# A gated mix of two attentions, forward and backward: who asks for the sweep's chunks in the backward weave, and what is loaded before it

## The chip, the core and the metric

The kernel runs on one core of one Trainium2 chip. The core has TensorE (PE, with PEld for its weight loads), VectorE (DVE), ScalarE (ACT), GpSimd (POOL) and SyncE (SP); SP issues most of the transfers here, GpSimd the rest. The metric is the device time of one execution in microseconds; the time of a kernel is the median of its runs.

## The reference

Two attention layers read the same input x (2048 tokens of 576), and a gate mixes them:

```python
g = sigmoid((x * gate_w).sum(-1, keepdims=True))
a = A(x)     # 32 query heads of 18, one shared key and value head, softmax over all 2048 keys, output projection
b = B(x)     # recurrent: segments of 32 tokens with 8 memory tokens ahead of them, 32 heads of 128
out = g * a + (1 - g) * b
```

In B each segment attends over its own 32 tokens (causal) and the 8 memory tokens; the first 8 rows of its output are the memory of the next of the 64 segments. The kernel returns the output and the gradients, for a given gradient of the output, of x, of the weights of A and B, of the first memory and of the gate: a forward pass and a full backward pass.

## The kernel before, in words

The program is one long sequence of stages: preparation and projections; a forward weave of B's recurrence with A's first pass; the token stage `b_bulk` (from about 2010 to 2604 us), which does attention and its gradients for B's own tokens; the backward weave (2604 to 4272 us); then `b_post`, the weight gradients `b_dw` and `a_final`. The order of the instructions on each engine is the order in which the program writes them (`manual_schedule`).

The backward weave is what the change is about. `weave` (L302 to 318) interleaves two generators. `a_pass2`, the sweep, goes over A's second pass in 1024 units (4 blocks of 512 keys, 256 units each). A unit is two score matmuls (`b_S`), an exponential on ScalarE (`b_E`), two gradient matmuls (`b_dP`), two products on VectorE (`b_dS`) and the accumulation into `b_acc`. Four units share one chunk of queries and output gradients, `b_QS`, 128 x 1024 values of bf16 (256 KB), loaded from `qs_dram`; there are 256 chunks in three buffers, `QS[c % 3]`. `load(c)` is written in the step n = 4c - 6 (L2107), and the chunk is first read by `mm_S(4c)`, which is written in step 4c - 1, five steps later. The first two chunks are loaded in the token stage by `sweep_first` (L2048), called at step `t == NG - 8`.

`b_chain_bwd`, the chain, goes backwards through B's 64 segments, with 16 yields in each, so 16 units and 4 chunks of the sweep run per segment. A segment needs the upstream rows `r_dOm` (from `dm` and the weights `WoT`), the spread probabilities `r_PqB` (from `r_pT` by `pad_in`, `pad_T` and `blocks`), loads of its own (`load_a`, `load_b`, `load_c`, on SP), and 24 weight pieces `WT` and the `WoT` pieces that stay in SBUF. It also computes, four blocks per segment, the key and value gradients of the token stage (`kv_load`, `kv_blk`, `kv_mm`, `kv_out`), whose results GpSimd stores (`dvx_dram`, `dkx_dram`, L1157). GpSimd also stores `pq_dram` (L1101), `dOm_dram` (L1198), `dTm_dram` (L1273), `dmT_dram` (L1174) and `dxr_dram` (L1318), and prepares blocks (`r_kb`, `r_dSB`, `r_dSqB`, `r_PqB`, `r_prod`, `r_hx`, `r_dspad`) that TensorE and VectorE read.

The weave begins with 12 lead steps of the sweep alone. At the lead steps named in `prime`, here 2 and 5, one piece of the chain is run too: step 2 runs the chain up to its first yield (buffers zeroed, `load_a` and `load_b` of the last segment), step 5 up to the second (`load_c`, with `r_dx` and `r_q`). What follows the second yield, `pad_in`, `r_PqB`, and in the last segment the zeroing of `r_dOm` and `x_rows`, comes after the lead. Each step also draws one item of `early`, here `bwd_weights` (L678): weight pieces 12 to 23, then the four `WoT` pieces and their tail, on SP. The pieces 0 to 11 are loaded in the token stage into the ring buffers that its own loads no longer need (`load`, L705).

Of the kernel before, what the change touches and what calls it, by code (L numbers as in the profile page):

```python
# [12 lines left out]
BF16 = mybir.dt.bfloat16  # L13
# [3 lines left out]
P = 128  # L17
# [5 lines left out]
E = 128  # L23
# [23 lines left out]
class Kern:  # L47
# [628 lines left out]
        self.WoT = (pool.tile([P, 4, J], BF16, name="WoT"), pool.tile([P, 4, 512], BF16, name="WoTt"))  # L676

    def bwd_weights(self, pool):  # L678
        for j in range(12, 24):
            self.load_WT(j, pool)  # L680
            yield
        for kt in range(4):
            self.nc.sync.dma_start(self.WoT[0][:, kt, :], self.st_WoT[kt])
            yield
        self.nc.sync.dma_start(self.WoT[1][:], self.st_WoTt[:])
        yield
# [6 lines left out]
    def b_bulk(self, wp, vp, kp, sp, psum):  # L693
        nc = self.nc
# [5 lines left out]
        NG = NTT * 8  # L700
        NC = NTT * 2

        self.WT = {}

        def load(c, names):  # L705
            if c >= NC:
                for w in names:
                    if w in deep and len(self.WT) < 12:
                        self.load_WT(len(self.WT), w=w)
                return  # L710
            tt, h0 = c // 2, 16 * (c % 2)
            d = C.setdefault(c, {})
            for w in names:
                if w == "mT":
                    if c % 2 == 0:
                        mT[tt] = {}
                        for x in ("k", "v"):
                            mT[tt][x] = kp.tile([P, 4, HB, 8], BF16, name=f"x_{x}mT", bufs=2)
                            nc.sync.dma_start(mT[tt][x][:], self.mTd[x][4 * tt:4 * tt + 4].rearrange("s p h t -> p s h t"))
                elif w in ("kB", "vB"):  # L720
                    for i in range(4):
                        nc.sync.dma_start(
                            mB[w[0]][c % 2][32 * i:32 * i + 32, :, i, :],
                            self.mtok[w[0]][tt * 32:(tt + 1) * 32, h0 * P:h0 * P + 2048]
                            .rearrange("r (g i e) -> r g i e", i=4, e=E)[:, :, i, :])
                else:
                    if w in deep:
                        d[w] = self.ring(w)[:, 0:2048].rearrange("p (h e) -> p h e", e=P)
                    else:
                        d[w] = vp.tile([P, 16, P], BF16, name=f"x_{w}", bufs=3)[:]  # L730
                    nc.sync.dma_start(d[w].rearrange("p h e -> p (h e)"),
                                      self.xtok[w][tt * P:(tt + 1) * P, h0 * P:h0 * P + 2048])

        deep = self.RING
# [229 lines left out]
        for t in range(NG + 6):  # L964
            if t == NG - 8:
                self.sweep_first()
            sc["D"] = psum.tile([P, 512], F32, name="x_D", bufs=1)
            sc["Sb"] = psum.tile([P, 512], F32, name="x_S", bufs=1)
            for n, st in order:
                if n is None:  # L970
                    st(t)
                    continue
                if 0 <= t - n < NG:
                    st(t - n)
                if st in after and t - n >= 0 and (t - n) % 4 == 3:
                    c = (t - n) // 4
                    for w, wait in after[st]:
                        later.setdefault(t + wait, []).append((c + (BQ if w in deep else 3 if w in ("mT", "v") else 2), (w,)))
                        if wait == 0:
                            load(*later[t].pop())  # L980
            first(t)
            if t % 4 == 2 and t // 4 - 2 in range(NTT // 4):
                self.dl_rows(t // 4 - 2, sp, psum)
            for x in later.pop(t, ()):
                load(*x)
            flush(t >= NG)
# [55 lines left out]
    def b_chain_bwd(self, wot, sp, kd, kvp, keep, psum):  # L1042
        nc = self.nc
# [121 lines left out]
        yield  # L1165
        pad_in("p", nxt["pT"][:, 1, :])
        PqB = blocks(pad_T("p"), "r_PqB")
        for s in reversed(range(NSEG)):
            L, nxt = nxt, {}
            d_ = dm[s % 2]  # L1170
# [1 line left out]
            n0 = 4 * (NSEG - 1 - s - 4)  # L1172
            kv_out(n0 - 1)
            nc.gpsimd.dma_start(self.dmT_dram[:, :, s, :], d_[:, 0:NKT, 0:8])  # L1174
            dOm = sp.tile([P, 8, E], BF16, name="r_dOm", bufs=1)
            if s == NSEG - 1:
                nc.gpsimd.memset(dOm[:], 0.0)
                x_rows(s, 0, pT[:, 0, :])
            else:
                pj = [psum.tile([P, 512], F32, name=nm, bufs=1) for nm in ("r_pj", "r_x")]  # L1180
            for k, parts in enumerate((((0, (0, 1, 2)),), ((0, (3, 4)), (1, (0, 1))), ((1, (2, 3, 4)),))):
                if s == NSEG - 1:
# [863 lines left out]
        dq_.dma_start(self.qs_blk(b, 1).rearrange("a p c -> p a c"), qt.rearrange("p a t x -> p a (t x)"))  # L2046

    def sweep_first(self):  # L2048
        self.QS = [self.wr.tile([P, 2, 512], BF16, name=f"b_QS{c}", bufs=1) for c in range(2)]
        self.KVb = [self.wr.tile([P, 512], BF16, name="b_KV0", bufs=1)]  # L2050
        self.nc.sync.dma_start(self.KVb[0][:], self.kv_dram[:, 0:512])
        for c in range(2):
            self.nc.sync.dma_start(self.QS[c][:], self.qs_dram[0, c])

    def a_pass2(self, keep, sp, kvp, psum):
# [7 lines left out]
                if kb:  # L2063
                    nc.sync.dma_start(KV[kb][:], self.kv_dram[:, kb * 512:kb * 512 + 512])

        self.QS.append(sp.tile([P, 2, 512], BF16, name="b_QS2", bufs=1))
        self.KVb.append(keep.tile([P, 512], BF16, name="b_KV1", bufs=1))
        load_KV(0)
        Q, S, E_, D_ = {}, {}, {}, {}
# [2 lines left out]
        def load(c):  # L2072
            if c < NC:
                p, q4 = (c // 4) % NPR, c % 4
                QS = self.QS[c % 3]
                if c > 1:
                    nc.sync.dma_start(QS[:], self.qs_dram[p, q4])
                Q[c] = (QS[:, 0, :], QS[:, 1, :].rearrange("p (a b) -> p a b", b=P))

        def pair(n):  # L2080
# [170 lines left out]
def build_full(tc, A_x, A_wq, A_wk, A_wv, A_wo, B_mem0, B_Wq, B_Wk, B_Wv, B_Wo, gate_w, grad_out, outs_raw,  # L2251
# [10 lines left out]
    with SB("const") as cpool, tc.tile_pool(name="dram", bufs=1, space=bass.MemoryType.DRAM) as dram:  # L2262
# [10 lines left out]
        with ExitStack() as man:  # L2273
            man.enter_context(tc.manual_schedule())
            k.dl_all = dlk.tile([P, k.NTT, 2, NPR, 2], BF16, name="a_dl")
            with SB("bw1") as bw1:
                k.alloc_W(bw1, ("k", "v"))
                prj = ExitStack()
                pds = prj.enter_context(SB("pds", RIGHT))
                for n in range(3):  # L2280
                    k.proj_load(items, n, pds)
                bwt = ExitStack()
                bwt_ = bwt.enter_context(SB("bwt"))
                with PS("wop") as wop:
                    k.make_WoT(bwt_, wop)
                pdp = prj.enter_context(PS("pdp"))

                def extra(n):
                    if 1 <= n <= 10:
                        k.load_W("kv"[(n - 1) // 5], (n - 1) % 5)  # L2290
                    if n >= 11:
                        k.qs_pads(n - 11, pds)
                k.b_proj(items, 0, n0, pds, pdp, extra)
                bwt.close()
                with SB("bw2") as bw2:
                    k.alloc_W(bw2, ("q",))
                    with SB("a2k") as a2k:
                        def extra(n):
                            if n < 27:
                                k.qs_pads(n - 11, pds)  # L2300
                            if n == n0:
                                for kt in range(NKT):
                                    k.load_W("q", kt)
                            elif n == len(items) - 6:
                                k.first_mem(a2k)
                            elif n == len(items) - 4:
                                k.load_A_kv(a2k)
                        k.b_proj(items, n0, len(items), pds, pdp, extra)
                        prj.close()
                        with SB("a2s") as a2s, SB("cfs") as cfs, PS("cfp") as cfp, PS("a2p") as a2p:  # L2310
                            k.weave(k.b_chain_fwd(a2k, cfs, cfp), k.a_pass1(a2k, a2s, a2p, cfp), 2)
            tw = ExitStack()
            k.wr = tw.enter_context(SB("wr"))
            with SB("xv") as xv, SB("xw") as xw, SB("xk") as xk, SB("xs") as xs, PS("xp") as xp:
                k.b_bulk(xw, xv, xk, xs, xp)
            wob.close()
            twp = tw.enter_context(SB("tw"))
            with SB("a3s", RIGHT) as a3s, SB("a3k", RIGHT) as a3k, SB("rw") as rw, SB("rs") as rs, \
                    SB("rd") as rd, SB("rk") as rk, SB("rv") as rv, PS("rp") as rp, PS("a3p") as a3p:
                k.weave(k.b_chain_bwd(rw, rs, rd, rv, rk, rp), k.a_pass2(a3k, a3s, rv, a3p), 12, (2, 5),  # L2320
                        k.bwd_weights(twp))
            wHs = ExitStack()
            wH = wHs.enter_context(SB("wH", RIGHT))
            with SB("yr", RIGHT) as yr, SB("ys") as ys, PS("yp") as yp:
                ht = k.b_post(ys, yr, wH, yp)
            tw.close()
# [81 lines left out]
```

## Time and profile before

| | us |
|---|---|
| median of 3 runs | 5256.78 (5253.13 to 5257.46) |
| profiled execution | 5281.87 |
| its span | 5280.2 |

The page's first part gives the share of the span in which each engine was busy, and its fourth the chain that ended last:

```profile
PE 4991.9 (95%) x90945; PEld 2895.7 (55%) x90945; DVE 3589.3 (68%) x7113; ACT 3278.5 (62%) x4753; POOL 2561.0 (49%) x4871
...
PE 28%; ACT 3%; issue 2%; DMA 1%; SPq 1%; POOL 0%; DVE 0%; POOLq 0%; DVEq 0%; ACTq 0%
```

TensorE is busy nearly all the time. The 40 slices show where it isn't, and how its clock and the DMA engines stand there; each slice is 132 us, so the backward weave takes the 20th to the 33rd:

```profile
PE   7999999999999998989789999999999999999999
...
PEclk9999999999999998999899999999999999999999
DMA  7765666666665547878857988989977769966663
```

How such rows are read: an instruction's row has its start, its duration, its engine and line, the tile that it writes and the tiles that it reads, and in brackets how long the engine stood idle before it and on what. A transfer's row on SP or POOL is the time of the issue alone; when the data came shows only in who waited for it.

### The profile page before, as it was taken

The numbers are of one execution on the slowest core, as the hardware profiler recorded it, in microseconds if no ns is written. First come the engines' busy times: TensorE is split into PE (matmuls) and PEld (weight loads), VectorE is DVE, ScalarE is ACT, GpSimd is POOL, SyncE is SP. The second block draws the span as 40 slices with busy tenths as digits, with TensorE's granted clock in tenths as the row PEclk, the third lists the DMA queues.
The fourth block names the chain that finished last, engine by engine and source line by source line (L and its number), as shares of the span: only waits on it lengthen the run. The fifth ranks groups of instructions, "written<-read, shape, count | busy, mean of one in ns | idle before, by whom it ended". The sixth has DMA issues, their size and how long they took to land. (4 is left out here: it accounts for less than half of the span.)

```text
span 5280.2 us, 213541 instructions
## 1 busy us (share of the span) xinstructions
PE 4991.9 (95%) x90945; PEld 2895.7 (55%) x90945; DVE 3589.3 (68%) x7113; ACT 3278.5 (62%) x4753; POOL 2561.0 (49%) x4871
## 2 busy tenths in 40 slices
PE   7999999999999998989789999999999999999999
PEld 4335555555555556777545555555554467764444
DVE  5338888888888887767688888888888831111212
ACT  4228888888888885666578888878877732110100
POOL 3005555555555556767646666666654321222213
PEclk9999999999999998999899999999999999999999
DMA  7765666666665547878857988989977769966663
GB/s 237 232 189 136 144 142 140 146 143 143 146 142 127 125 110 216 246 236 251 271 158 177 196 194 194 194 189 201 203 164 143 149 161 227 285 222 213 197 187 106
DMA packets 1122571, 961.24 MB, mean 182 GB/s; under 512 B 691006, under 2 KB 950535, under 8 KB 1112398
## 3 DMA queue, kind: packets, MB, share of 16 engines
q1 hardware_dynamic: 1022174, 707.69, 55.7%
q0 software_dynamic: 99296, 239.73, 15.3%
q8 instruction: 712, 11.67, 1.0%
q14 instruction: 245, 2.01, 0.1%
q10 hardware_dynamic: 144, 0.15, 0.0%
HBM read 522.81 MB, written 357.96 MB: 167 GB/s over the span
## 5 line engine op out<-in xcount | busy, mean ns | idle before, releaser
L2119 DVE TENSOR_TENSOR b_dS<-b_dP,b_E 128x512 bf16<-128x512 f32 x2048 | 1315.3, 684 | 231.5 <-issue 98.7
L1951 DVE TENSOR_TENSOR a_W<-a_dP,a_E 128x512 bf16<-128x512 f32 x2048 | 1314.1, 684 | 206.0 <-issue 76.7
L2096 ACT ACTIVATE b_E<-b_S 128x1024 bf16<-128x1024 f32 x1024 | 1047.7, 1023 | 296.8 <-PE b_dP L82 206.8
L1913 ACT ACTIVATE a_E<-a_S 128x1024 bf16<-128x1024 f32 x1024 | 1049.0, 1024 | 273.9 <-PE a_dP L82 194.4
L82 PEld LDWEIGHTS <-b_QS 32*128 32x128 bf16 (+1 forms) x8192 | 270.1, 92 | 535.2 <-issue 467.2
L82 PE MATMUL r_pj<-WT,r_dT 128*32 128x288 bf16 x12288 | 496.8, 287 | 6.6 <-issue 6.6
L82 PE MATMUL b_S<-b_KV,b_QS 32*128 32x512 bf16 x2048 | 406.4, 384 | 102.0 <-ACT b_E L2096 60.4
L82 PE MATMUL w_acc<-w_d,w_h 128*128 128x512 bf16 (+1 forms) x2400 | 475.0, 379 | 0.0
L82 PE MATMUL a_S<-a_QD,l_KV 32*128 32x512 bf16 x2048 | 399.7, 381 | 46.0 <-ACT a_E L1913 20.1
L82 PE MATMUL b_acc<-b_dS,b_QS 128*32 128x512 bf16 x2048 | 425.6, 394 | 0.2
L82 PE MATMUL a_acc<-a_E,l_VK 128*32 128x256 bf16 x8192 | 413.6, 278 | 6.9 <-issue 1.9
L82 PE MATMUL b_acc<-b_E,b_QS 128*32 128x512 bf16 x2048 | 407.7, 395 | 0.0
L82 PE MATMUL b_dP<-b_KV,b_QS 32*128 32x512 bf16 x2048 | 404.0, 389 | 0.0
L82 PE MATMUL a_dP<-a_QD,l_KV 32*128 32x512 bf16 x2048 | 398.6, 386 | 0.0
L82 PEld LDWEIGHTS <-r_dT 128*32 128x32 bf16 x12288 | 336.9, 97 | 96.0 <-issue 9.7
L82 PEld LDWEIGHTS <-w_h 128*128 128x128 bf16 (+1 forms) x2688 | 229.3, 100 | 258.9 <-issue 9.7
L82 PEld LDWEIGHTS <-l_KV 32*128 32x128 bf16 x4096 | 154.5, 91 | 307.2 <-issue 279.9
L82 PE MATMUL a_acc<-a_W,l_WK 128*32 128x256 bf16 x4096 | 292.0, 274 | 0.0
L79 ACT CAST w_o<-w_acc 128x512 bf16<-128x512 f32 x54 | 31.6, 585 | 384.7 <-PE w_acc L82 374.9
L82 PEld LDWEIGHTS <-l_VK 128*32 128x32 bf16 x8192 | 129.3, 94 | 237.4 <-issue 233.5
L1132 POOL TENSOR_TENSOR r_kb<-r_ks,bmask 128x512 bf16<-128x512 bf16 x176 | 188.6, 1072 | 131.7 <-DMA r_ks<-dsx_dram 47.0
L77 DVE CAST w_o<-w_acc 128x512 bf16<-128x512 f32 x54 | 37.4, 692 | 313.4 <-PE w_acc L82 290.7
(492 smaller groups left out, 10560.5 us busy)
## 6 DMA issues: line engine op xcount, KB each, us to landing
b_QS<-qs_dram SPq DMA_DIRECT2D x256, 256.0 KB
dOx_dram<-p_tok SPq DMA_DIRECT2D x16, 1024.0 KB
c_vx<-vx_dram SPq DMA_DIRECT2D x64, 256.0 KB
krow_dram<-c_k POOLq DMA_DIRECT2D x64, 256.0 KB
qrow_dram<-c_q POOLq DMA_DIRECT2D x64, 256.0 KB
vrow_dram<-c_v POOLq DMA_DIRECT2D x64, 256.0 KB
x_q<-qx_dram SPq DMA_DIRECT2D x32, 512.0 KB
x_k<-kx_dram SPq DMA_DIRECT2D x32, 512.0 KB
```

The source lines that it names most:

```text
L77: nc.vector.tensor_copy(out, in_)
L79: nc.scalar.copy(out, in_)
L82: return self.nc.tensor.matmul(out, lhsT, rhs, start=start, stop=stop, tile_position=tp, skip_group_check=True)
L1132: nc.gpsimd.tensor_tensor(out=B[:], in0=a[:].unsqueeze(2).to_broadcast([P, 4, 4, SEG]), in1=self.bmask[:, :, 0].unsqueeze(1).unsqueeze(3). ...
L1913: nc.scalar.activation(E_[n][:], S.pop(n)[:], ACT.Exp, scale=SCALEA)
L1951: nc.vector.tensor_tensor(out=W_[n][:, i, :], in0=dP[i][:], in1=E_[n][:, i, :], op=ALU.mult)
L2096: nc.scalar.activation(E_[n][:], S.pop(n)[:], ACT.Exp, scale=SCALEA)
L2119: nc.vector.tensor_tensor(out=D_[n][:, i, :], in0=dP[i][:], in1=E_[n][:, i, :], op=ALU.mult)
```

## The change

Four edits:

- `sweep_first` loads three chunks instead of two in the token stage. The third buffer, `QS[2]`, moves from the sweep's pool to the pool `wr`, which is open already then.
- All later chunks (253) are asked for by GpSimd (`nc.gpsimd`) instead of SP. Where each stands in GpSimd's order follows from the place of `load(c)` in the program, which is unchanged.
- `prime` is (2, 5, 9): the third piece of the chain (`pad_in`, `r_PqB`, the zeroing of `r_dOm`, `x_rows` of the last segment) ends in a yield of its own and runs after lead step 9. `dOm` is allocated there for the last segment, and in the loop for the others.
- Weight pieces 12 and 13 are loaded in the token stage, at steps NG - 15 and NG - 11, into the pool `wr`; `bwd_weights` begins with piece 14, so that the pieces after them and the `WoT` pieces come two steps earlier. A counter `n_ring` takes the place of `len(self.WT)` in counting the pieces in the ring buffers.

```diff
     def bwd_weights(self, pool):
-        for j in range(12, 24):
+        for j in range(14, 24):
             self.load_WT(j, pool)
             yield
...
         self.WT = {}
+        self.n_ring = 0
...
-                    if w in deep and len(self.WT) < 12:
-                        self.load_WT(len(self.WT), w=w)
+                    if w in deep and self.n_ring < 12:
+                        self.load_WT(self.n_ring, w=w)
+                        self.n_ring += 1
...
             if t == NG - 8:
                 self.sweep_first()
+            if t % 4 == 1 and 0 <= (t - NG + 16) // 4 < 2:
+                self.load_WT(12 + (t - NG + 16) // 4, self.wr)
...
         pad_in("p", nxt["pT"][:, 1, :])
         PqB = blocks(pad_T("p"), "r_PqB")
+        dOm = sp.tile([P, 8, E], BF16, name="r_dOm", bufs=1)
+        nc.gpsimd.memset(dOm[:], 0.0)
+        x_rows(NSEG - 1, 0, nxt["pT"][:, 0, :])
+        yield
         for s in reversed(range(NSEG)):
...
-            dOm = sp.tile([P, 8, E], BF16, name="r_dOm", bufs=1)
-            if s == NSEG - 1:
-                nc.gpsimd.memset(dOm[:], 0.0)
-                x_rows(s, 0, pT[:, 0, :])
-            else:
+            if s < NSEG - 1:
+                dOm = sp.tile([P, 8, E], BF16, name="r_dOm", bufs=1)
                 pj = [psum.tile([P, 512], F32, name=nm, bufs=1) for nm in ("r_pj", "r_x")]
...
     def sweep_first(self):
-        self.QS = [self.wr.tile([P, 2, 512], BF16, name=f"b_QS{c}", bufs=1) for c in range(2)]
+        self.QS = [self.wr.tile([P, 2, 512], BF16, name=f"b_QS{c}", bufs=1) for c in range(3)]
...
-        for c in range(2):
+        for c in range(3):
             self.nc.sync.dma_start(self.QS[c][:], self.qs_dram[0, c])
...
-        self.QS.append(sp.tile([P, 2, 512], BF16, name="b_QS2", bufs=1))
...
-                if c > 1:
-                    nc.sync.dma_start(QS[:], self.qs_dram[p, q4])
+                if c > 2:
+                    nc.gpsimd.dma_start(QS[:], self.qs_dram[p, q4])
...
-                k.weave(k.b_chain_bwd(rw, rs, rd, rv, rk, rp), k.a_pass2(a3k, a3s, rv, a3p), 12, (2, 5),
+                k.weave(k.b_chain_bwd(rw, rs, rd, rv, rk, rp), k.a_pass2(a3k, a3s, rv, a3p), 12, (2, 5, 9),
                         k.bwd_weights(twp))
```

## The prediction

> **What bounds the kernel now.** I read the chain that ended last first (TensorE has most of it), then the stretches around the changed stage, then what TensorE waits for in it, and last the rows around those waits. Columns of the first view: busy time of each engine and its count, the granted TensorE clock, the DMA share, GB/s.
>
> ```profile
> core 0: us, PE busy (x) PEld busy (x) DVE busy (x) ACT busy (x) POOL busy (x), PEclk, DMA share, GB/s
> 2240.00:2604.00 364.00, 337.02 (x7726) 273.85 (x7727) 262.79 (x891) 231.35 (x495) 262.59 (x414) 0.99 0.82 246
> 2604.00:2680.00 76.00, 45.94 (x767) 19.15 (x766) 42.25 (x72) 37.11 (x45) 29.38 (x50) 0.69 0.85 265
> 3400.00:3800.00 400.00, 384.29 (x8197) 210.40 (x8185) 341.49 (x592) 327.49 (x437) 259.75 (x420) 0.99 0.90 196
> ...
> ```
>
> The backward weave runs from 2604 to 4272. In its middle TensorE is busy 384 of 400 us: only waits can be won there. Its first 76 us are another matter: 46 us busy, at a clock of 0.69. The waits of TensorE, for the first 86 us of the weave and then for the rest (total, times, longest):
>
> ```profile
> PE b_S L82 <- DMA b_QS<-qs_dram: 17.1, 4, 9.3
> PE b_S L82 <- ACT b_E L2096: 10.1, 17, 1.3
> PE r_x L82 <- POOL r_dOm L1177: 3.7, 1, 3.7
> ```
>
> ```profile
> PE b_S L82 <- ACT b_E L2096: 50.3, 177, 2.1
> PE b_S L82 <- DMA b_QS<-qs_dram: 13.9, 15, 2.4
> ```
>
> So sweep chunks that land late cost 31 us, more than half of it in four waits at the start; that is the ceiling of what earlier chunks can give, beside 3.7 us for the zeroing of r_dOm. The b_E waits are the sweep's own pace and stay.
>
> **The start, part by part.** TensorE and then SP's queue (start, duration, what it waited for):
>
> ```profile
> 2618.81 0.61 PE L82 MATMUL b_S<-b_KV,b_QS 32*128 32x512 bf16 x2 [1.37 <-DMA b_QS<-qs_dram]
> ...
> 2634.60 0.61 PE L82 MATMUL b_S<-b_KV,b_QS 32*128 32x512 bf16 x2 [9.32 <-DMA b_QS<-qs_dram]
> 2639.50 0.39 PE L82 MATMUL r_x<-seln,r_dOm 128*128 128x32 bf16 x8 [3.73 <-POOL r_dOm L1177]
> ...
> 2665.22 0.61 PE L82 MATMUL b_S<-b_KV,b_QS 32*128 32x512 bf16 x2 [6.22 <-DMA b_QS<-qs_dram]
> ...
> 2673.94 0.39 PE L82 MATMUL b_S<-b_KV,b_QS 32*128 32x512 bf16 x2
> ```
>
> ```profile
> 2607.92 0.96 SPq L2077 DMA_DIRECT2D b_QS<-qs_dram  x1
> ...
> 2618.43 1.39 SPq L1036 DMA_DIRECT2D WT<-st_WT  x3
> 2620.05 0.33 SPq L1076 DMA_DIRECT2D r_dx<-dmx_dram  x1
> ...
> 2620.90 0.42 SPq L1036 DMA_DIRECT2D WT<-st_WT  x1
> 2625.84 0.34 SPq L2077 DMA_DIRECT2D b_QS<-qs_dram  x1
> 2626.27 5.29 SPq L1036 DMA_DIRECT2D WT<-st_WT  x4
> ...
> 2652.58 0.38 SPq L2077 DMA_DIRECT2D b_QS<-qs_dram  x1
> ...
> ```
>
> ```profile
> 2637.07 0.62 POOL L281 TENSOR_TENSOR r_PqB<-r_pq,bmask 128x256 bf16<-128x256 bf16 x1 [16.52 <-DVE r_pq L1090]
> ...
> 2638.38 1.06 POOL L1177 MEMSET r_dOm<- 128x1024 bf16 x1
> ```
>
> Chunk 2 is asked for at 2607.92 and used at 2618.81. Chunk 3 is asked for only at 2625.84, because SP stands behind weight pieces, and comes 8.8 us later. Chunk 6 is asked for at 2652.58 and comes 12.6 us later. These 8.8 to 12.6 us are what one transfer takes while the weights stream.
>
> (a) Chunk 2 loaded in the token stage: the 1.37 us go.
>
> (b) Chunk 3 on GpSimd, which has nothing to do between its memsets and 2637 (a wait of 16.52 for r_pq): it can be asked for once chunk 0, whose buffer it takes, is used up, which is before chunk 2's first use at 2618.81: at least 7 us before SP did it. The 9.32 us go.
>
> (c) The third chain piece within the lead: r_PqB and the memset (0.62 and 1.06 us on GpSimd) run beside lead steps 10 to 12, so the 3.73 us go. Without that cover they would cost the same 3.7 us again.
>
> What is late next: with 1.37, 9.32 and 3.73 gone TensorE would be at the row of 2639.50 by 2625.1, and just behind it the first segment multiplies r_dx. That load was asked for at 2620.05, behind three weight pieces, and none of the four edits asks for it before the lead's first steps do. With the 8.8 to 12.6 us of its neighbours it lands (estimate) at 2628.9 to 2632.7; with two weight pieces fewer at the front I take 2631.6. So of 14.4 us 7.9 are won, bounds 6.8 and 10.6, and 14.4 if r_dx is no longer late at all.
>
> (d) Two WT pieces moved into the token stage, three chunks instead of two before the weave. They are 576 KB each (the profile's list of transfers), with the chunk 1.4 MB that leave a stretch running at 265 GB/s: 5.3 us of transfers. This is what brings chunk 6 in: asked for on a queue without weight pieces ahead of it, it needs to come 6.2 us sooner. I take 5.5 of 6.22 us, bounds 0 and 6.2. Behind that wait TensorE runs at half speed: the four units from 2665.22 to 2673.94 take 8.72 us, where four take 6.24 in the rows below. Those 2.5 us go with the stall; I take 2.
>
> Sum of the start: 7.9 + 5.5 + 2 = 15.4 us, between 7 and 23.
>
> The price in the token stage: 1.4 MB more in a stretch with a DMA share of 0.82 and 246 GB/s is 5.7 us of transfers, and TensorE is 337 of 364 us busy there. It hides in the free share unless a token tile comes later; bounds 0 and 5.7, and I take 1, since no edit puts them ahead of a load due within the same step.
>
> **The steady part.** One segment: GpSimd's queue, SP's chunks, and the first use of each chunk on TensorE.
>
> ```profile
> 3628.28 0.94 POOL L1101 DMA_DIRECT2D pq_dram<-r_xq  x1
> 3630.61 0.67 POOL L1195 TENSOR_TENSOR r_prod<-r_dOT,r_oT 128x256 bf16<-128x256 bf16 x1 [1.40 <-ACT r_dOT L1193]
> ...
> 3634.69 0.23 POOL L1086 COPY r_dspad<-r_dS 128x64 bf16<-128x64 bf16 x1
> 3635.72 0.60 POOL L1157 DMA_DIRECT2D dvx_dram<-r_kvo  x1 [0.80 <-ACT r_kvo L1156]
> ...
> 3640.42 0.75 POOL L1273 DMA_DIRECT2D dTm_dram<-r_dTc  x1
> 3642.01 0.56 POOL L1157 DMA_DIRECT2D dkx_dram<-r_kvo  x1 [0.84 <-ACT r_kvo L1156]
> ```
>
> ```profile
> 3623.82 0.41 SPq L2077 DMA_DIRECT2D b_QS<-qs_dram  x1
> ...
> 3626.64 0.81 SPq L2077 DMA_DIRECT2D b_QS<-qs_dram  x1
> ...
> 3635.36 0.42 SPq L2077 DMA_DIRECT2D b_QS<-qs_dram  x1
> ...
> 3639.06 0.38 SPq L2077 DMA_DIRECT2D b_QS<-qs_dram  x1
> ```
>
> ```profile
> 3628.76 0.39 PE L82 MATMUL b_S<-b_KV,b_QS 32*128 32x512 bf16 x2 [0.20 <-DMA b_QS<-qs_dram]
> ...
> 3635.00 0.39 PE L82 MATMUL b_S<-b_KV,b_QS 32*128 32x512 bf16 x2
> ...
> 3641.28 0.39 PE L82 MATMUL b_S<-b_KV,b_QS 32*128 32x512 bf16 x2
> ...
> 3647.51 0.39 PE L82 MATMUL b_S<-b_KV,b_QS 32*128 32x512 bf16 x2 [0.21 <-ACT b_E L2096]
> ```
>
> Four units take 6.24 us (3628.76 to 3635.00). In the changed program's order on GpSimd the four chunks of a segment stand between pq_dram and r_prod, between r_dspad and dvx_dram, between dTm_dram and dkx_dram, and between dvx_dram and r_hx.
>
> ```profile
> 3621.68 0.58 POOL L1157 DMA_DIRECT2D dvx_dram<-r_kvo  x1 [1.52 <-ACT r_kvo L1156]
> 3623.43 0.20 POOL L1300 COPY r_hx<-r_hs 64x32 bf16<-64x32 bf16 x1 [1.17 <-DVE r_hs L1299]
> ```
>
> GpSimd's own cost: an issue of 0.58 us, as dvx_dram has it, falls into idle gaps of 1.40, 0.80, 0.84 and 1.17 us. So 253 issues cost nothing on the path; without the gaps they would be 2.3 us per segment on an engine busy 260 of 400 us. An issue first waits for its buffer. The chunk that used it last ends seven units, 10.9 us, ahead of the first use of the new one, and GpSimd reaches the issues at most 6.6 us ahead of it: no wait, so r_prod, dvx_dram, dkx_dram and r_hx behind them are not held.
>
> What each chunk gets from the call to its first use, SP before and GpSimd after:
> - first: 3626.64 to 3635.00, 8.4 us; from the end of pq_dram at 3629.22, 5.8 us
> - second: 3635.36 to 3641.28, 5.9 us; from 3634.92, 6.4 us
> - third: 3639.06 to 3647.51, 8.5 us; from the end of dTm_dram at 3641.17, 6.3 us
> - fourth: 3623.82 to 3628.76, 4.9 us and late; from 3622.26, 6.5 us
>
> The gain is the fourth: its 1.6 us more is above the mean of the 15 steady waits (13.9/15 = 0.93), and only the longest (2.4) outlast it. I take 11 of 13.9 us, bounds 7 (half, if a few long ones make up most) and 13.9.
>
> The price is the first and third, 2.6 and 2.2 us less time. The trace bounds their landing from above only (8.4 and 8.5, no wait seen). The fourth took 4.9, and the second under 5.9, in the same traffic. If the first and third take no longer, nothing is late; if they take all of their time, each segment loses 4.8 us. dvx_dram and dkx_dram, the heavy part of that traffic, last 45 segments:
>
> ```profile
> L1157 POOL DMA_DIRECT2D dvx_dram<-r_kvo x88: 581/592/608, 2755.8 to 3874.6; - x88
> ```
>
> (1119 us at 25 us a segment.) So 0 to 215 us. I take the value near the two rows that are known: a quarter of the segments late by 0.93, as 15 of some 60 were late with 4.9 us: 45/4 x 0.93 = 10 us, 9 of them from the third, which stands right behind dTm_dram in GpSimd's queue.
>
> The Trainium skill ("DMA: Bandwidth & Descriptors", section "Anatomy of one DMA — SWDGE (gpsimd) path") fits a transfer asked for by GpSimd as about 2.0 us plus its bytes over 436e3 per us, which is an estimate of 2.6 us for 256 KB. By it no chunk would be late and the 10 us were 0. The rows above have 4.9 us on SP's queue in this traffic, so I keep my value.
>
> **Sum.** -15.4 (start) - 11 (fourth chunk) + 10 (first and third) + 1 (token stage) = -15.4 on the profiled execution's 5281.87 us (span 5280.2), that is 5266.5. The profiled execution is 25 us above the median of the runs, 5256.78; the waits are the same work there, so I carry the difference over: 5241 us.
>
> **The rivals.**
>
> 1. Slower: GpSimd's queue is the worse place for a chunk. The mechanism is the steady price above: chunks wait behind dTm_dram, dOm_dram and dvx_dram of their own queue, in a DMA share of 0.90. At 6.5 us from call to landing the first is late by 0.7, the second by 0.1, the third by 0.16: 0.96 x 45 = 43 us in place of 10, so 33 more than the forecast, +17.6, 5274 us. It decides from about 6.35 us on, where the lateness of a segment, some 0.55 us, eats the 25 us won. For it: first and third were never asked to land in under 8.4. Against: the second chunk does it in 5.9 us every segment.
>
> 2. The start is bound by transfers, not by who asks. 265 GB/s and a share of 0.85 stand for 76 us; then chunk 3 goes early, r_dx, r_q and the weights go late, and the gain is that of the moved 1.4 MB alone, 4 to 5 us: -4.5 - 11 + 10 + 1, 5252 us. For it: r_dx, as computed, is the next to be waited for. Against: SP asked for nothing from 2621.3 to 2625.8, so the order of calls matters too. The Trainium skill (same page, "Rules for kernel authors") says that spreading transfers over SP, ACT and GpSimd gives no bandwidth and saves only issue time; that speaks for this rival.
>
> 3. Nothing is late on GpSimd's queue (latencies near 4 us): -15.4 - 13.9 + 1, 5228 us. For it: the 4.9 and 5.9 above include the DMA transposes that SP's queue has around its chunks. Against: the same engines serve both queues. The fit of the Trainium skill cited above gives this rival.
>
> 4. The change doesn't do what it says: the waits are hidden again by the b_E waits and the clock, since 50 us of them stand on the same matmul. Then 5257 us. Against: a wait is put down to what came last, and 9.32 us is no b_E wait.
>
> **How the numbers follow.** Differences below 0.2%, 10.5 us, can't be told from none here. Forecast 0.42 (its own range 5231 to 5251; 0.34 of it below 5246.3); rival 1 0.24 (0.20 slower by over 0.2%, 0.03 within, 0.01 faster); rival 2 0.16 (0.12 within, 0.04 faster); rival 3 0.14 (faster); rival 4 0.04 (0.03 within, 0.01 slower). Faster 0.53, same 0.26, slower 0.21. The range: 5224 takes in rival 3 with a few us more at the start; 5278 takes in rival 1 at 6.5 us, and leaves its worse end out.
>
> **What will show it.** Right: no wait for b_QS above 1 us before 2650, one wait for r_dx of 3 to 8 us near 2626, the 6.2 us gone, fewer than 8 steady waits on the chunk used behind r_hx, some 10 new ones on the third. Wrong: b_QS waits spread over first and third chunks with a sum above 40 us (rival 1); a start as long as before with other names on the waits (rival 2); GpSimd's r_prod, r_hx or r_dSqB turning up as what TensorE waits for, which would mean that the gaps did not hold the issues; or a token stage longer by over 3 us.

## The result, and the profile after

The changed kernel is slower: 5288.74 us against 5264.06 us, medians of 7 runs each, a ratio of 1.0046 with a 95% interval of 1.0033 to 1.0059, or some 24 us. Forecast was 5241 us, 15 us faster.

The profiled execution of the changed kernel took 5288.74 us, with a span of 5286.9. Beside the first profile of the kernel before (span 5280.2) that is 6.7 us more, not 24: that profile was of an execution 18 us above its kernel's median, and a part of the text below is about that.

First the start. What TensorE waits for from 2600 to 2690 in the changed kernel (total, times, longest):

```profile
PE b_S L82 <- ACT b_E L2100: 11.6, 21, 1.3
PE b_dP L82 <- DVE b_dS L2123: 8.4, 1, 8.4
PE r_pj L82 <- DMA r_dx<-dmx_dram: 7.7, 1, 7.7
```

The four waits for b_QS (17.1 us) and the one for r_dOm (3.7) are gone, the wait for r_dx is there as forecast, and one that was not forecast has come: b_dP for b_dS, 8.4 us. Its rows on TensorE, VectorE, GpSimd and SP:

```profile
2632.06 0.21 PE L82 MATMUL r_pj<-perm,r_dx 128*128 128x32 bf16 x1 [7.71 <-DMA r_dx<-dmx_dram]
...
2658.25 0.58 PE L82 MATMUL b_dP<-b_KV,b_QS 32*128 32x512 bf16 x1 [8.45 <-DVE b_dS L2123]
```

```profile
2657.18 0.45 DVE L1094 STREAM_TRANSPOSE r_pq<-r_ppad 128x256 bf16<-128x256 bf16 x1 [9.06 <-POOL r_ppad L1090]
```

```profile
2656.91 0.24 POOL L1090 COPY r_ppad<-r_pT 128x64 bf16<-128x64 bf16 x1 [12.74 <-DMA r_pT<-pm_dram]
```

```profile
2630.12 4.08 SPq L683 DMA_DIRECT2D WoT<-st_WoT  x4
...
2636.73 11.63 SPq L1067 DMA_TRANSPOSE r_vxT<-vx_dram  x1
2648.41 0.58 SPq L1069 DMA_DIRECT2D r_pT<-pm_dram  x1
```

Read from below: the WoT pieces, two steps earlier than before, stand four in a row ahead of the second segment's loads. The issue of r_vxT takes 11.63 us behind them (3.78 before), r_pT is asked for at 2648.41 and lands at 2656.9, GpSimd copies it, VectorE transposes it, and only then come the products b_dS that wait behind the transpose. The first 32 units of the sweep take 73.3 us, from 2602.3, where they took 75.7 from 2604.5.

Then the rest of the weave, from 2690 to 4275:

```profile
PE b_S L82 <- ACT b_E L2100: 48.6, 178, 0.5
PE b_S L82 <- DMA b_QS<-qs_dram: 33.6, 33, 3.3
...
PE r_pj L82 <- POOL r_hx L1305: 1.0, 1, 1.0
PE r_x L82 <- issue: 0.5, 1, 0.5
PE r_x L82 <- POOL r_prod L1200: 0.5, 2, 0.3
```

Chunks are late by 33.6 us where they were by 13.9. Which ones shows the chain of waits; two stretches of it, 234 us apart (start, duration, what):

```profile
3009.31 0.66 POOL dTm_dram L1278
3009.97 7.68 DMA b_QS<-qs_dram
...
3243.98 0.66 POOL dTm_dram L1278
3244.63 8.94 DMA b_QS<-qs_dram
```

It is the third chunk of a segment, asked for directly behind dTm_dram. Put to each chunk by its landing in the trace's completion records, from the ninth chunk to the 200th, the third is late 32 times in 48 for 31.0 us together, the fourth once for 2.2, the first and second never. Before, the fourth was late 14 times for 13.6 us. From call to landing the third takes 6.6 us (median), the first 3.7, the second 3.5, the fourth 4.6.

The other engines are not it: r_hx and r_prod, which GpSimd's issues could have pushed back, cost 1.5 us together.

### The profile page after: what moved, and what is told of

Same layout as the page of the kernel before. It is cut to its first block, busy times and chain, and to the rows that moved or that the text cites. A ratio compares the mean times of both kernels' runs of the same rounds, so it can differ in the third digit from the quotient of the medians.

```text
span 5286.9 us, 213607 instructions
## 1 busy us (share of the span) xinstructions
PE 4988.4 (94%) x90945; PEld 2890.9 (55%) x90945; DVE 3591.7 (68%) x7113; ACT 3279.8 (62%) x4753; POOL 2698.8 (51%) x5124
## 4 chain that ended last, share of the span: by engine, by line
PE 63%; ACT 11%; issue 8%; DMA 7%; POOL 5%; DVE 4%; SPq 0%; POOLq 0%; ACTq 0%; DVEq 0%
PE w_acc L82 12%; PE a_S L82 7%; ACT a_E L1918 6%; PE a_acc L82 6%; PE c_pj L82 6%; DMA b_QS<-qs_dram 5%; ACT b_E L2100 4%; PE b_S L82 4%; PE p_pb L82 4%; PE r_pj L82 4%; PE c_x L82 3%; PE r_x L82 3%; PE b_acc L82 3%; PE x_tr L87 2%; PE x_po L82 1%
## 5 line engine op out<-in xcount | busy, mean ns | idle before, releaser
L82 PEld LDWEIGHTS <-hm 128*32 128x32 bf16 x7680 | 194.1, 97 | 84.0 <-issue 10.8
```

Source lines behind the costliest of these rows:

```text
L82: return self.nc.tensor.matmul(out, lhsT, rhs, start=start, stop=stop, tile_position=tp, skip_group_check=True)
```

## The experiments

Times are ratios to the kernel before, run on the same chip in the same session, with their 95% interval. The sessions ran on different chips, and the median of the kernel before lay between 5262.0 and 5275.93 us in them, so ratios are compared and not microseconds. "Steady waits" are TensorE's waits for b_QS after 2690. The letters of theories and rivals are those of the expectations.

**Chunks back on SP.** The edits at the start stay.

```diff
-                    nc.gpsimd.dma_start(QS[:], self.qs_dram[p, q4])
+                    nc.sync.dma_start(QS[:], self.qs_dram[p, q4])
```

> The changed kernel, but the chunks after the third are asked for by SP again; the other three edits stay. Theory T (the loss is the third chunk of each segment, which lands behind dTm_dram on GpSimd's queue; 18 such waits of together 17 us): the steady waits of TensorE for b_QS fall from 33.6 us to about the 14 of before, on the fourth chunk again; time about 15 to 20 us below the changed kernel, near before. Rival U (the 253 issues on GpSimd delay GpSimd's own outputs, and TensorE loses there): the same fall here, so this run alone doesn't tell T from U. Rival V (the loss comes from the weights and r_pT at the start or from the token stage): no fall in steady, time as the changed kernel.

0.9997 (0.9984 to 1.0009); steady waits 5.9 us. The whole loss goes with the queue. The three other edits are then worth nothing that can be measured; but on SP the chunks of the start are late again (18.0 us of waits before 2690, where the kernel before had 17.1), so this run doesn't price those edits with the chunks on GpSimd.

**Third chunk alone back on SP.**

```diff
-                    nc.gpsimd.dma_start(QS[:], self.qs_dram[p, q4])
+                    (nc.sync if c % 4 == 2 else nc.gpsimd).dma_start(QS[:], self.qs_dram[p, q4])
```

> The changed kernel, with only the third chunk of each segment (c % 4 == 2) asked for by SP, the other three by GpSimd. Theory T: the third gets its 8.5 us back and the fourth keeps its 6.5, so steady b_QS waits fall from 33.6 us to under 6; time 25 to 30 us below the changed kernel, 5 to 10 below before. Rival U (GpSimd's issues as such): three quarters of the issues are still there, so at most a quarter of the loss goes, 5 us or less, and the waits stand on r_prod, r_hx or r_dSqB. Rival V: as the changed kernel.

0.9996 (0.9983 to 1.0008); steady waits 6.3 us, and those on r_prod 0.5. One chunk in four carries the loss, so GpSimd's issues as such (U) are not the cause of it. But the gain of 5 to 10 us below before was not there.

**Weights back at their steps**, alone and with the third chunk on SP.

```diff
     def bwd_weights(self, pool):
+        for _ in range(2):
+            yield
         for j in range(14, 24):
```

> The changed kernel with two empty steps ahead of weight piece 14, so that the remaining weight pieces and the WoT pieces are asked for at the steps at which before asked for them. Theory W (the 8.4 us wait of b_dP for b_dS near 2658 is r_pT of the next segment, asked for behind four WoT pieces in a row and 11.6 us of r_vxT's issue; VectorE stands at the transpose of r_ppad): that wait falls below 3 us, the steady part stays as in the changed kernel; time 5 to 8 us below it. Rival X (the start is bound by transfers, the order does not matter): a wait of 6 us or more turns up elsewhere before 2680 and the start is no shorter.

> Both: the third chunk of each segment on SP, and two empty steps ahead of weight piece 14. Theories T and W together: the sum of both gains, 30 to 38 us below the changed kernel and 8 to 15 below before. Rivals U and X: no more than 5 us below the changed kernel.

1.0034 (1.0022 to 1.0047) and 0.9997 (0.9984 to 1.0009). The b_dP wait stays at 7.0 and 5.4 us; in the first a wait of 1.4 us for WoTt comes too, in the second one of 9.8 us for a chunk. Theory W failed in this form: two steps were not enough to get r_pT ahead; in the first of the two kernels r_vxT's issue in front of it still took 9.41 us.

**Second profiles of both kernels, and the one edit alone** (`c > 1` on GpSimd in the kernel before).

> The kernel before, unchanged, for a second profile. The profile on which the prediction rests was of an execution of 5281.87 us, 17 us above the median of 35 runs (5264.86). If the waits at the start and on the fourth chunk are the same in every execution, this profile has some 17 us of b_QS waits before 2690 and some 14 after, as the first. If they differ from run to run (theory R), an execution near the median has a weave some 15 us shorter, and the waits that the prediction counted as gains are in part not there: steady waits under 7 us.

> The changed kernel, unchanged, for a second profile. If the third chunk is late in every execution (theory T), the steady b_QS waits are again 25 to 40 us, nearly all on the third chunk; if they came from that one execution (theory R applied to the changed kernel), they are below 15.

> The kernel before with one edit alone: every chunk from the third on (c > 1) is asked for by GpSimd. Theory T: steady b_QS waits of 30 us or more on the third chunk, and the time 15 to 25 us above before; the other three edits of the change then are worth nothing together. If those edits hid a part of the loss or added to it: below 10 or above 35 us.

The changed kernel has 36.1 us of steady waits again, nearly all on the third chunk (33.6 us from the ninth to the 200th chunk). The kernel before has 16.7 us at the start again, as in the first profile, and 8.1 after it. So the waits at the start came twice and the steady ones differ. But theory R was about an execution near the median, and this one, 5295.44 us, is 20 us above the median of its own session (5275.93): R isn't tested by it. Fewer late chunks didn't make it short: after its first 32 units the sweep took 1594.2 us, in the first profile, of another session, 1580.4. The edit alone gives 1.0054 (1.0037 to 1.0072), 31.2 us of steady waits and the third chunk late by 27.6. So the third chunk of theory T is confirmed; that it is late because it stands behind dTm_dram is tested further down. From 1.0054 to the 1.0046 of the whole change are 4 us, with some 12 us either way (an estimate from the two intervals): the three other edits neither hide nor add anything that can be told.

**The order at the start**: load_c at lead step 3, and the WoT pieces six steps later, each with the third chunk on SP.

```diff
-... 12, (2, 5, 9),
+... 12, (2, 3, 9),
```

> The third chunk of each segment on SP, and the lead's second chain piece (load_c with r_dx and r_q) at step 3 instead of step 5, so that r_dx is asked for ahead of all but one of the weight pieces from 14 on. Theory O (the order of the calls sets the start): the wait for r_dx (7.7 to 8.9 us) falls below 3 and the first 32 units of the sweep take 5 us less than the 74.8 of the kernel with only the third chunk on SP; the time falls by 4 to 6 us. Rival X (the start is bound by transfers): the wait turns up on another tile before 2690 and the first 32 units take 72 us or more; time unchanged.

```diff
             self.load_WT(j, pool)
             yield
+        for _ in range(6):
+            yield
         for kt in range(4):
```

> The third chunk on SP, and six empty steps between the last WT piece and the first WoT piece, so that the second segment's load_a (with r_pT) is asked for ahead of the WoT pieces. Theory W' (r_pT behind the WoT pieces holds VectorE and so TensorE, 5.4 to 8.4 us in every variant so far): the wait of b_dP for b_dS falls below 1 us and the first 32 units of the sweep take under 69 us, against 73 to 75 in the variants with the third chunk on SP; time 4 to 8 us below the kernel with only the third chunk on SP. Rival X (transfers bound the start): the first 32 units stay above 71 us with the wait on another tile, or the WoT pieces are waited for before 2700.

1.0005 (0.9993 to 1.0017) and 0.9997 (0.9986 to 1.0008). In the first the wait for r_dx falls from 8.9 to 3.3 us and the one for a chunk grows from 2.9 to 5.2; the first 32 units take 73.6 us. In the second the wait of b_dP for b_dS is gone, so its cause is shown; in its place stand 2.4 and 1.8 us for WoT and WoTt beside 6.8 for r_dx, and the first 32 units take 70.0. The signs of rival X came in both: the order of the calls chooses which tile is waited for, and the time stays. That what has to be moved sets the length of the start is not shown: with the same loads the first 32 units took 73.3 and 67.8 us in the two profiles of the changed kernel, and 66.1 with the weights back at their steps.

**Why the third chunk is slow: its place in the queue, or the time of the call?** The chunk on GpSimd ahead of dTm_dram, and the chunk on SP one step later.

```diff
-                if n % 4 == 2:
+                if n % 4 == (1 if n // 4 % 4 == 0 else 2):
                     load(n // 4 + 2)
```

> The changed kernel with the third chunk of each segment asked for on GpSimd one sweep step earlier, which puts it directly ahead of dTm_dram in GpSimd's order instead of directly behind it; some 0.7 us earlier in time. Theory Q (it is late because it stands behind dTm_dram in its own queue): the steady b_QS waits, 33.6 and 36.1 us in two profiles of the changed kernel, fall below 10, and the time falls by 15 us or more below the changed kernel. Theory C (it is late because the call comes 2.1 us later than SP's did, and a transfer called at that place takes 6 to 8 us on either queue): 0.7 us more take off a third to two thirds, 12 to 24 us of waits stay, and the time falls by 5 to 14 us.

```diff
-                if n % 4 == 2:
+                if n % 4 == (3 if n // 4 % 4 == 0 else 2):
                     load(n // 4 + 2)
```

> The kernel with the third chunk on SP (its steady waits 6.3 us, its time that of before), with that chunk asked for one sweep step later, so about as late as GpSimd's call in the changed kernel, but on SP's queue and not behind dTm_dram there. Theory Q: still hardly late, steady b_QS waits below 10 us, time within 0.2% of before. Theory C: the waits are back, 20 us or more, on the third chunk, and the time is 10 to 25 us above before.

The second run came out as theory Q said, the first as neither did. Ahead of dTm_dram the kernel is much slower, 1.0096 (1.0078 to 1.0114); late on SP costs nothing, 0.9999 (0.9988 to 1.001). TensorE's waits after 2690, of the first and then of the second:

```profile
PE b_S L82 <- DMA b_QS<-qs_dram: 26.2, 15, 4.4
PE r_pj L82 <- issue: 13.1, 10, 3.4
PE b_S L82 <- issue: 5.1, 2, 3.4
```

```profile
PE b_S L82 <- DMA b_QS<-qs_dram: 9.8, 9, 3.6
```

In the first the chunk takes 6.4 us (median) and over 10.5 in five cases of 48: fewer late chunks, each longer, and 18 us in which TensorE waits for nothing that the profile shows. Why it is worse by as much as that stays open. In the second the chunk takes 6.0 us, with 7.1 from call to use (medians); in the changed kernel 6.6 and 6.7.

The first run rules out more than its time says. Its chunk has 8.2 us from call to use, nearly the 8.6 that SP gave it in the kernel before, and is late 14 times in 48, there 3 times. So the later call and the place directly behind dTm_dram can't be the whole of it: in GpSimd's queue the chunk is late with an early call and ahead of that store too. What in that queue does it, the runs don't show.

**What makes any transfer slow there.** Just ahead of that place SP asks for r_kx, whose access pattern has a slowest dimension of 4. In four loads of 32 rows each:

```diff
-            nc.sync.dma_start(L["kx"][:].rearrange("p u e -> p (u e)"),
-                              self.xtok["k"][s * 32:(s + 1) * 32, :].rearrange("r (c x) -> c r x", c=4))
+            for c in range(4):
+                nc.sync.dma_start(L["kx"][32 * c:32 * c + 32].rearrange("p u e -> p (u e)"),
+                                  self.xtok["k"][s * 32:(s + 1) * 32, 1024 * c:1024 * c + 1024])
```

> The changed kernel with the load of r_kx (256 KB, called 4 us ahead of the third chunk; its completion is counted from 5 DMA engines where the other loads have 16) made as four loads of 32 rows each. Theory K (r_kx holds a third of the DMA engines for 6 us, and the third chunk's share on those engines waits behind it): the third chunk lands within 5 us of its call instead of 6.7 (median), the steady b_QS waits fall from 34 and 36 us to under 10, and the time falls by 20 us or more, to before or below. Rival B (the sum of bytes called there is what takes the time, on whichever engines): the chunk still takes 6 us or more, waits 20 us or more, time within 8 us of the changed kernel.

> The kernel before with r_kx in four loads. There the third chunk has 8 us and is not late, the fourth is late by 8 to 14 us in sum. Theory K: the fourth chunk, the r_k, r_ks and r_kr loads land sooner; steady waits fall to under 8 us, time 0 to 10 us below before. Rival B: nothing measurable, or slower by a few us, since SP issues three more transfers per segment.

> The third chunk on SP and r_kx in four loads. If the time of before is bound by waits that are left (theory K), this is the fastest so far, 5 to 15 us below before. If nothing is left to win in the weave once no chunk is late (theory L), it is within 0.2% of before, as the kernel with only the third chunk on SP was.

The kernel before with this edit alone has the lowest ratio of the study: 0.9954 (0.9939 to 0.9969), 5244.65 us, a larger gain than was expected of it; its steady waits are 8.8 us. The changed kernel with it is at 1.0023 (1.0007 to 1.004) and keeps 29.1 us of steady waits, so theory K failed there; with the third chunk on SP it is at 0.9978 (0.9963 to 0.9992). r_kx took 6.5 us in the kernel before and takes 2.9 a piece; r_k behind it went from 6.4 to 3.0, the third chunk on SP from 6.2 to 4.7. On GpSimd, behind dTm_dram, the chunk still takes 6.2 us although dTm_dram itself went from 5.6 to 4.1. So both are shown: r_kx slows what is called behind it, and GpSimd's queue is worse than SP's for a chunk called at the same place, by 1.5 us here and by 0.8 in the last experiment below.

**The remaining gap.** All with r_kx in four loads: the changed kernel with the chunks on SP; the kernel before with only the fourth, and with only the third chunk on GpSimd (the edit shown is the last one's).

```diff
-                    nc.sync.dma_start(QS[:], self.qs_dram[p, q4])
+                    (nc.gpsimd if c % 4 == 2 and c > 2 else nc.sync).dma_start(QS[:], self.qs_dram[p, q4])
```

> The changed kernel with all chunks after the third on SP, and r_kx in four loads: only the edits at the start and r_kx differ from before. If those edits are worth nothing, as without the split, the ratio to before is that of the kernel before with r_kx split, 0.994 to 0.997. If they cost or gain, below 0.993 or above 0.998.

> The kernel before with r_kx in four loads and only the fourth chunk of each segment on GpSimd. Its steady waits of 6 us on the fourth chunk go; if they are worth their size, the ratio to before is 0.992 to 0.995, else (another wait takes their place, or a chunk on GpSimd costs as such) 0.9954 or more.

> The kernel before with r_kx in four loads and only the third chunk of each segment on GpSimd, directly behind dTm_dram. Theory P (GpSimd's queue is the worse place for this one chunk, whoever else uses it): the chunk takes 6 us or more where it took 4.7 on SP, steady b_QS waits of 20 us or more, and the time rises by 15 us or more above the same kernel with it on SP, to a ratio of 0.998 or more. Rival M (it takes all four chunks on GpSimd together): ratio below 0.9965 and waits below 12 us.

0.9956 (0.994 to 0.9973), 0.998 (0.9968 to 0.9993) and 1.0016 (1.0004 to 1.0028). The edits at the start, with the chunks on SP, are worth nothing once more. The third chunk alone on GpSimd costs 1.0016 - 0.9954 = 0.62%, 33 us, the fourth alone 0.26%; the 0.9954 is of another session, and against the 0.9956 of this one it is 0.60 and 0.24%. The third alone took 5.4 us, less than theory P's 6, and all waits for chunks were 17.9 us, less than 20, 11.4 of them on the third; the time it cost is more than they are. Their waits after 2690, third and fourth:

```profile
PE b_S L82 <- DMA b_QS<-qs_dram: 17.9, 17, 3.2
...
PE r_pj L82 <- POOL r_hx L1301: 2.2, 3, 1.0
```

```profile
PE r_pj L82 <- POOL r_hx L1301: 5.3, 5, 1.1
PE b_S L82 <- DMA b_QS<-qs_dram: 4.2, 3, 2.4
...
PE r_x L82 <- POOL r_prod L1196: 2.6, 3, 1.1
```

With the fourth on GpSimd, TensorE waits for r_hx, which GpSimd writes directly behind that issue: 5.3 us, gone in the kernel without it. In four of the five cases GpSimd has stood some 2 us ahead of that issue until TensorE let it go on, as here:

```profile
3159.08 0.54 POOL L2078 DMA_DIRECT2D b_QS<-qs_dram  x1 [1.98 <-PE r_x L82]
3159.62 0.22 POOL L1301 COPY r_hx<-r_hs 64x32 bf16<-64x32 bf16 x1
```

There the issue does not fit into its gap, and rival U is right in the small.

## Why the prediction was wrong, step by step

- **The third chunk, the step that failed.** The place was right: GpSimd's queue, and in it the third chunk (rival 1). The forecast gave the first and third 10 us, nine of them to the third, and the third cost 31.0 us in the profile. The price was read from the wrong rows: the fourth chunk's 4.9 us and the second's 5.9. The third's own transfer took 6.2 us on SP already, hidden under 8.6 us from call to use; the trace's rows bounded it only from above, and the rows that were used were of transfers called at other places of the segment. It had 6.3 us left and took 6.6. A better row was there: r_k, called by SP 1.6 us ahead of it, took 6.4 us. The reason given, its place right behind dTm_dram, can't be the whole one: ahead of dTm_dram it was late as well. Rival 1's sum, 43 us at 6.5 us a chunk, had the size, but laid most of it on the first chunk, which was never late (3.7 us).
- **The fourth chunk**: 11 us forecast, 13.6 to 2.2 in the first pair of profiles, so right there; 8.3 to 1.2 in the second pair.
- **The start**: 15.4 us forecast. The first 32 units won 2.4 us in one pair of profiles and 6.5 (74.3 to 67.8) in the other, and the runs can't tell the edits from nothing (1.0046 with them beside 1.0054 with the chunks on GpSimd alone, where the first 32 units took 70.5 us). This is the second step that failed. With 31 us in place of the nine the prediction's sum is 6.6 us above before (-15.4 - 11 + 32 + 1); without the 15.4 it is 22, and the runs have some 24. The wait for r_dx was right: forecast until 2631.6, measured 2632.06 in a weave that began 2.3 us earlier. The 5.5 us and the half-speed stretch behind chunk 6 were wrong: a wait of 8.4 us came in their place, through r_pT behind the WoT pieces, with half speed around it (granted clock 0.50 from 2655 to 2668). The prediction moved those pieces two steps and did not follow them past load_a in SP's queue. Rival 2 forecast 4 to 5 us for the start.
- **The token stage**: 1 us forecast; the weave's first b_S came at 2602.3 and 2604.1, before at 2604.5 and 2603.6. No price is seen, but 1 us can't be told: over all profiles this matmul comes between 2592.6 and 2610.2.
- **GpSimd's issues in its gaps**: right for the total (1.5 us of waits in the changed kernel), not for r_hx where other waits are gone. That an issue never waits for its buffer was wrong: GpSimd stands at the fourth chunk's issue for b_acc, which reads that buffer, 17 times for 49.0 us after 2690, all in segments without dvx_dram.
- **From the profile to the median.** The prediction carried the difference over as if both executions had the same waits in them. Both profiled executions of before lie 18 to 20 us above the medians of their sessions, so what a usual one waits for is not on record. After its first 32 units the sweep took 1580.4 and 1594.2 us in them, 1589.9 and 1602.3 in the changed kernel: the profiles show 8 to 10 us there of the 24. A part of what varies is half speed (next but one section).

## What to carry to other kernels

A transfer that nobody waits for tells only an upper bound of its time, so before giving up its lead, price it from the transfers called beside it in the same microseconds, and look at how many DMA engines the loads just ahead of it use: splitting one such load gained 0.46% here, and no choice of queue gained anything against the kernel before. When a load is moved earlier in an in-order queue, follow what now stands behind it until somebody waits.

## What the runs showed of the hardware

**A load on few engines holds up the next.** For r_kx the trace has 5 completion records, the first 1.0 us after the issue; most loads have 16. The Trainium skill ("DMA: Bandwidth & Descriptors", section "Why a DMA increments its semaphore by 16 and not by 1") has a transfer from SP run on the largest number of engines up to 16 that divides both slowest dimensions, and the count jump by the missing ones at once. That is 4 engines here and 1 + 4 records: it agrees, and the expectations above, which say 5 engines, are to be read as 4. Split, each piece has 16 records. The same page of the Trainium skill says in its section "Rules for kernel authors" that a slowest dimension under 16 confines the whole load to at most that many engines; that its neighbours pay too is what the runs add: the four loads move the same rows and bytes.

**A wait costs more than its length.** In the changed kernel, TensorE's rows around one late third chunk:

```profile
3249.72 0.39 PE L82 MATMUL b_S<-b_KV,b_QS 32*128 32x512 bf16 x2
3253.62 0.39 PE L82 MATMUL b_S<-b_KV,b_QS 32*128 32x512 bf16 x2 [2.56 <-DMA b_QS<-qs_dram]
3255.20 0.57 PE L82 MATMUL b_S<-b_KV,b_QS 32*128 32x512 bf16 x2
3257.54 0.61 PE L82 MATMUL b_S<-b_KV,b_QS 32*128 32x512 bf16 x2
3259.55 0.39 PE L82 MATMUL b_S<-b_KV,b_QS 32*128 32x512 bf16 x2
```

After 2.56 us of waiting the sweep runs at half speed: the granted clock is 0.50 from 3255.3 to 3258.6, and the two units from 3255.20 take 4.35 us and not 3.1. Counting stretches in which the sweep's matmuls last over 0.5 us, after 2690: 3 of together 15.2 us in the first profile of before (5281.87 us) and 8 of 37.8 in the second (5295.44); 8 of 25.5 and 13 of 46.4 in the two of the changed kernel; 16 of 67.0 with the chunk ahead of dTm_dram; 1 of 1.2 in before with r_kx split. The stretch from 3000 to 3400, in before and in before with r_kx split (the columns are those of the prediction's first view):

```profile
3000.00:3400.00 400.00, 378.95 (x8106) 207.25 (x8102) 336.68 (x583) 323.26 (x431) 258.15 (x418) 0.99 0.90 194
```

```profile
3000.00:3400.00 400.00, 388.61 (x8352) 213.32 (x8340) 348.01 (x603) 334.20 (x447) 266.56 (x430) 1.00 0.88 200
```

246 more matmuls fit into the same 400 us, at a granted clock of 1.00 in place of 0.99. That the half speed makes up most of the spread between executions of one kernel is an inference from two pairs of profiles. Between kernels it does not order the times: the changed kernel with r_kx split has 5 such stretches of 11.7 us and took 5288.76 us. The times of the runs without a profile can't be split.
